# Attention scores of halves three to eight as two row tiles of the array, and a new order of the attention pieces

## The chip, the cores and the metric

The kernel runs on one core of a Trainium2 chip. The metric is the device time of one execution in microseconds; where several runs are given, it is their median. Before the change it is 242.2 us (three runs, 242.13 to 242.77). The profiled execution, from which all other times here are taken, has a span of 239.8 us.

Engines are called by the names of the profile: PE is the matrix engine (PEld its weight loads), ACT the engine for exponentials and other functions, DVE the vector engine, POOL the general engine, SP the queue that issues transfers.

## The reference

Attention over a window of 96 keys and 8 global keys, with a bias by distance, for 4 batches of 8 heads, 768 positions and 64 dimensions to a head; then a gated feed-forward (512 to 1536 to 512) over all 3072 rows.

```python
scores = (q @ k.T) / sqrt(64) + bias          # [4, 8, 768, 768]
keep   = (key < 8) | (0 <= row - key < 96)
a      = softmax(where(keep, scores, -1e9))
x      = (a @ v) as [3072, 512]
out    = (max(x @ w_gate, 0) * (x @ w_val)) @ w_out
```

## The kernel before

The work goes in eight halves (s = 0 to 7) of 384 rows: half of one batch's positions, all 8 heads. Halves 0 and 1 have a path of their own. From half 2 on, the attention of half c+1 is woven into the feed-forward of half c: a list of feed-forward items, each about 0.65 us of PE, and a list of attention pieces that are dropped between them at given fractions of the way.

The heads are handled in four pairs (p = 0 to 3). kT[b][p] holds the keys of both heads of a pair, head 0 in partitions 0 to 63 and head 1 in 64 to 127, as stationary matrices of 128 columns for each block j of keys. The queries of a pair are held twice in qTb, each copy with the other head's partitions set to zero, so that one product over all 128 partitions gives the scores of both heads side by side:

```python
qTb = [const.tile([128, HP, 2, QH], BF16, name=f"qT{i}") for i in range(2)]   # d, pair, head, row
qz  = [const.tile([128, NN, HP, 2, 128], BF16, name=f"qz{i}") for i in range(2)]  # zero-padded, before the transpose

def piece_qk(s, p, g, later=None):
    ...
    qd = qTb[s % 2][:, p].rearrange("d e (n p) -> d e n p", n=NN)
    bank = banks_of_half[half][g]                 # one or two blocks of keys
    ps = qk_psum.tile([128, 512], FP32, name="qk_ps")
    ...
    for j, a, w, m in bank:
        n_ = 2 * NN * w
        nc.tensor.matmul(ps[:, c : c + n_], lhsT=kt[:, j, :],
                         rhs=qd[:, :, :, a : a + w], start=True, stop=True)
        c += n_
    nc.scalar.activation(es[:, 0:cols], ps[:, 0:cols], AF.Exp, bias=0.0, scale=scale)
    ...                                           # piece_mask multiplies es by m_all, on DVE
```

A pair takes three such banks. Their products have 432, 432 and 288 + 48 columns in an even half, and 144 + 336, 384 + 96 and 432 in an odd half.

The product with the values is taken for one head at a time. Its output has the 64 value columns and, in the other 64 partitions, the sum of the weights; the reciprocal comes by a logarithm and an exponential, for both heads together:

```python
def piece_av(s, p, e):
    av = av_psum.tile([128, 512], FP32, name="av_ps")
    ...                                           # 4 (even) or 5 (odd) matmuls
    nc.scalar.activation(ln[o0 : o0 + 64], av[d0 : d0 + 64, 0:QH], AF.Ln, bias=0.0, scale=1.0)
    if e == 1:
        ...
        nc.scalar.activation(rc, ln, AF.Exp, bias=0.0, scale=-1.0)
        piece_norm(s, p, 0)                       # DVE: xT = av * rc, head 0; head 1 by a later piece
```

PSUM has eight banks: three for scores (qk_psum), two for these products (av_psum), three for the feed-forward (ff_psum). A bank is written again only when its last reader is done. The order of the attention pieces, and where they stand:

```python
        QK = lambda p: [(0.18, lambda g=g: qk(p, g)) for g in range(3)]
        AV = lambda p: [(0.29, lambda e=e: (flush(), piece_av(s, p, e))) for e in range(2)]
        N = lambda p: [(0.0, lambda: piece_norm(s, p, 1))]
        g = QK(3)
        a = AV(2)
        return (QK(0) + QK(1) + AV(0) + N(0) + QK(2) + AV(1) + N(1) + g[0:1] + a[0:1] + g[1:3] + a[1:2]
                + N(2) + [(0.0, lambda: None)] * 2 + AV(3) + N(3))
    ...
    placed.append(spread(attention_pieces(c + 1), 0.0, 0.88 if c + 2 < NHALF else 0.8))
```

The feed-forward of a half is 24 items (12 of gate, 12 of val, each four matmuls of 384 columns) and then, for half 6, seven items p1, p2, p4, p6, p5, p7, p3 of six matmuls of 256 columns (two row tiles multiplied in seven products in place of eight); halves 3 to 5 have four items of three matmuls of 512 columns ahead of these. Their results are combined on DVE from the PSUM banks b (p1), a (p2 and p6), d (p4 and p5), c (p7 and p3):

```python
            def p6():
                self.product(st["a"], DH, ss(2), tt(2))
                add(st["o"][:, 0:2], two(st["a"]), st["o"][:, 2:3].to_broadcast([128, 2, DH]))
            def p5():
                self.product(st["d"], DH, ss(1), tt(1))
                add(st["o"][:, 2:4], two(st["d"]), st["o"][:, 1:2].to_broadcast([128, 2, DH]))
            ...
            def p3():
                self.product(st["c"], DH, ss(4), bb(1, 1))
                second(st["c"][:, 0:DH])          # an add of 512 columns, and a store
                add(st["o"][:, 3], st["c"][:, DH:], st["o"][:, 3])
```

Halves 0 and 1 take the values' product in another form (piece_av_wide): stationary matrices of 64 columns, so that the products of the two heads lie in the left and right half of the array (128 x 64 in the profile's names). It is the only place, besides the transposes of half 1, where the kernel before uses a part of the array at a time.

Of the kernel before, what the change touches and what calls it, by code (L numbers as in the profile page):

```python
# [8 lines left out]
FP32 = mybir.dt.float32  # L9
BF16 = mybir.dt.bfloat16  # L10
FP16 = mybir.dt.float16
# [5 lines left out]
def kernel(  # L17
# [51 lines left out]
    es_pool = ctx.enter_context(tc.tile_pool(name="es", bufs=3))  # L69
# [17 lines left out]
    kT = [[const.tile([128, NT, 128], BF16, name=f"kT{i}_{p}") for p in range(HP)] for i in range(2)]  # L87
    qTb = [const.tile([128, HP, 2, QH], BF16, name=f"qT{i}") for i in range(2)]
    kNb = [const.tile([128, HP, QH], BF16, name=f"kN{i}") for i in range(2)]
    qz = [const.tile([128, NN, HP, 2, 128], BF16, name=f"qz{i}") for i in range(2)]  # L90
    kc = [const.tile([128, NN, DM], BF16, name=f"kc{i}") for i in range(2)]

    obuf = const.tile([128, 2, 5, DM // 2], FP32)
# [149 lines left out]
    def warm_up(n):  # L243
        wps = ff_psum.tile([128, 512], FP32, name="ff_ps")
        for _ in range(n):
            nc.tensor.matmul(wps, lhsT=warm, rhs=warm.unsqueeze(1).to_broadcast([128, 4, 128]), start=True, stop=True)

    xT_of = {}
    es_of = {}
    es01_of = {}  # L250
    av_of = {}

    cast_of = {}
# [91 lines left out]
    def piece_exp(s, p, g):  # L345
        if p == HP - 1:

            es = kNb[s].rearrange("d p t -> d (p t)")[:, 480 * g : 480 * (g + 1)]
        else:
            if g == 0:  # L350
                es01_of[s, p] = es_pool.tile([128, 2, 480], BF16, name="es01")
            es = es01_of[s, p][:, g] if g < 2 else es_pool.tile([128, 480], BF16, name="es2")
# [5 lines left out]
        nc.scalar.activation(es[:, 0:c], qk_of[s, p][g][:, 0:c], AF.Exp, bias=0.0, scale=scale)  # L358
# [3 lines left out]
        for g in range(3):  # L362
            piece_exp(s, p, g)

    def piece_cast_k(s, p):
        nc.gpsimd.tensor_copy(  # L366
            kc[s % 2].rearrange("t n (h d) -> t h n d", d=D)[:, 2 * p : 2 * p + 2],
            ks_of[s][:, 2 * p : 2 * p + 2, :].rearrange("t e (n d) -> t e n d", n=NN))

    def piece_cast_q(s, p):  # L370

        qsrc = qs_of[s][:, 2 * p : 2 * p + 2, :].rearrange("t e (n d) -> t e n d", n=NN)
        for e in range(2):
            nc.gpsimd.tensor_copy(qz[s % 2][:, :, p, e, 64 * e : 64 * e + 64], qsrc[:, e])

    def piece_xk(s, n):
        nc.sync.dma_start_transpose(
            out=kNb[s % 2][:, :, n * 128 : (n + 1) * 128], in_=kc[s % 2][:, n])

    def piece_xq(s, n):  # L380
        nc.sync.dma_start_transpose(
            out=qTb[s % 2].rearrange("d p e t -> d (p e) t")[:, :, n * 128 : (n + 1) * 128],
            in_=qz[s % 2][:, n].rearrange("t p e z -> t (p e z)"))

    def piece_order(s, p):
        b, half = divmod(s, 2)
        put_keys(nc.gpsimd.tensor_copy, nc.gpsimd.tensor_copy, kT[b % 2][p], kNb[s % 2][:, p], half)

    def early_pieces(s):
        out = [(0.0, lambda p=p: piece_cast_k(s, p)) for p in range(HP)]  # L390
        out += [(0.0, lambda n=n: piece_xk(s, n)) for n in range(NN)]
        out += [(0.0, lambda p=p: piece_cast_q(s, p)) for p in range(HP)]
        out += [(0.0, lambda n=n: piece_xq(s, n)) for n in range(NN)]
        out += [(0.0, lambda p=p: piece_order(s, p)) for p in range(HP)]
        return out

    def piece_qk(s, p, g, later=None):
        b, half = divmod(s, 2)
        kt = kT[b % 2][p]
        qd = qTb[s % 2][:, p].rearrange("d e (n p) -> d e n p", n=NN)  # L400
        bank = banks_of_half[half][g]
        cols = sum(2 * NN * w for _, _, w, _ in bank)
        ps = qk_psum.tile([128, 512], FP32, name="qk_ps")
        if g == 0:
            es01_of[s, p] = es_pool.tile([128, 2, 480], BF16, name="es01")
        es = es01_of[s, p][:, g] if g < 2 else es_pool.tile([128, 480], BF16, name="es2")
        c = 0
        for j, a, w, m in bank:
            n_ = 2 * NN * w
# [23 lines left out]
    def piece_av(s, p, e):  # L433
        b, half = divmod(s, 2)
        h = 2 * p + e
        vb = vbuf[b % 2]
        av = av_psum.tile([128, 512], FP32, name="av_ps")
        av_of[s, p, e] = av
        av3 = av[:, 0:QH].rearrange("d (n p) -> d n p", n=NN)
        todo = [t for bank in banks_of_half[half] for t in bank]  # L440
        for i, (j, a, w, m) in enumerate(todo):
            es, c = es_of[s, p, j, e]
            z0 = 2 * D * h + (D if e == 0 else 0)
            nc.tensor.matmul(av3[:, :, a : a + w],  # L444
                             lhsT=vb[:, j, z0 : z0 + 128],
                             rhs=es[:, c : c + NN * w].rearrange("k (n p) -> k n p", n=NN),
                             start=(i == 0), stop=(i == len(todo) - 1),
                             skip_group_check=True)
# [4 lines left out]
        nc.scalar.activation(ln[o0 : o0 + 64], av[d0 : d0 + 64, 0:QH], AF.Ln, bias=0.0, scale=1.0)  # L453
        if e == 1:
            if s not in xT_of:
                xT_of[s] = xt_pool.tile([128, N_DC, QH], BF16, name="xT")
            rc = rc_pool.tile([128, QH], FP32, name="rcp")
            nc.scalar.activation(rc, ln, AF.Exp, bias=0.0, scale=-1.0)  # L458
            av_of[s, p, "r"] = rc
            piece_norm(s, p, 0)  # L460
# [43 lines left out]
    def piece_mul_wide(s, p):  # L504
        if s not in xT_of:
            xT_of[s] = xt_pool.tile([128, N_DC, QH], BF16, name="xT")
        nc.vector.tensor_tensor(xT_of[s][:, p, :], av_of[s, p][1][:, 0:QH], av_of[s, p, "r"], op=ALU.mult)  # L507

    def attention_pieces(s):
        masks = []  # L510

        def qk(p, g):
            ready = masks[:]
            masks.clear()
            piece_qk(s, p, g, masks)
            for f in ready:
                f()

        def flush():
            for f in masks:  # L520
                f()
            masks.clear()

        QK = lambda p: [(0.18, lambda g=g: qk(p, g)) for g in range(3)]
        AV = lambda p: [(0.29, lambda e=e: (flush(), piece_av(s, p, e))) for e in range(2)]
        N = lambda p: [(0.0, lambda: piece_norm(s, p, 1))]
        g = QK(3)
        a = AV(2)
        return (QK(0) + QK(1) + AV(0) + N(0) + QK(2) + AV(1) + N(1) + g[0:1] + a[0:1] + g[1:3] + a[1:2]
                + N(2) + [(0.0, lambda: None)] * 2 + AV(3) + N(3))  # L530


    out_v = out.rearrange("(s p n) d -> s n p d", p=128, n=NN)
# [156 lines left out]
    def ffn_pieces(c):  # L690
# [63 lines left out]
        if c == NHALF - 2:  # L754
            return f1, pair.items({"1": late[0:2], "2": late[2:4]})

        space = qz[0].rearrange("t n p e z -> t (n p e z)").bitcast(FP16)
# [35 lines left out]

    for h in range(H):
        setup_sid(h)
    QKB, FFB, AVB = (qk_psum, "qk_ps"), (ff_psum, "ff_ps"), (av_psum, "av_ps")

    def AV(s, p, *pools):
        piece_av_wide(s, p, *pools)
        piece_norm_wide(s, p)  # L800
# [133 lines left out]
    for i in range(2):  # L934
        nc.gpsimd.memset(qz[i].rearrange("t n p e z -> t (n p e z)").bitcast(mybir.dt.uint32), 0)
    for j in range(NT):
        fill_ones(nc.gpsimd, 1, j)
    for p in range(HP):
# [3 lines left out]
    def T2_piece(p):  # L942
        piece_t(2, p, *QKB, apart=True)
        piece_copy_k(2, p)
        piece_copy_q(2, p, nc.scalar.copy)

    T2 = [(0.0, lambda p=p: T2_piece(p)) for p in range(HP)]
    weave(f1_1[G[0]] + f1_0[G[1]][4:] + f1_1[G[1]],
# [3 lines left out]
          spread(T2, 0.55, 0.95))  # L952
    sums_wo = [(0.0, f) for i in (0, 3) for f in weight_sums(i, i + 3)]
    weave(f1_0[G[2]] + f1_1[G[2]] + f2_0 + f2_1,
          spread(attention_pieces(2), 0.02, 0.8), spread(early_pieces(3), 0.1, 0.76),
          spread(sums_wo, 0.42, 0.76))
# [46 lines left out]
```

The softmax here doesn't subtract the row's maximum and nothing guards it: scores larger than these inputs give would overflow.

## Time and profile before

| | us |
|---|---|
| time, median of 3 | 242.2 |
| span of the profile | 239.8 |
| PE busy | 232.1 (97%) |
| DVE busy | 174.8 (73%) |
| ACT busy | 154.3 (64%) |
| POOL busy | 95.6 (40%) |
| score matmuls (qk_ps from qT and kT), 118 | 26.6 busy |
| exponentials of scores, 78 | 40.9, 534 ns each |
| mask products, 118 | 32.9, 322 ns each |
| gate and val matmuls, 768 | 155.4 busy, 326 ns each |

Busy time of a matmul contains its way through the array, which overlaps the next one; what a matmul costs PE is the distance from its start to the next start. PE's clock is granted in full during the whole span, but for its first slices.

### The profile page before, as it was taken

The numbers are of one execution on the slowest core, as the hardware profiler recorded it, in microseconds if no ns is written. First come the engines' busy times: TensorE is split into PE (matmuls) and PEld (weight loads), VectorE is DVE, ScalarE is ACT, GpSimd is POOL, SyncE is SP. The second block draws the span as 40 slices with busy tenths as digits, with TensorE's granted clock in tenths as the row PEclk, the third lists the DMA queues.
The fourth block names the chain that finished last, engine by engine and source line by source line (L and its number), as shares of the span: only waits on it lengthen the run. The fifth ranks groups of instructions, "written<-read, shape, count | busy, mean of one in ns | idle before, by whom it ended". The sixth has DMA issues, their size and how long they took to land.

```text
span 239.8 us, 5192 instructions
## 1 busy us (share of the span) xinstructions
PE 232.1 (97%) x1859; PEld 155.9 (65%) x1859; DVE 174.8 (73%) x443; ACT 154.3 (64%) x328; POOL 95.6 (40%) x213
## 2 busy tenths in 40 slices
PE   7889999999999999999999999999999999999992
PEld 3676756666558666766658666676658666866682
DVE  6878676767877778585985778675985867964783
ACT  7899856878662787548754787547764888433300
POOL 8998935915590068103484066502460000000000
PEclk9999999999999999999999999999999999999999
DMA  6999999997989946938569756929451200020004
GB/s 171 197 173 185 205 282 261 171 103 253 129 178 148 305 122 133 93 94 258 92 112 128 224 159 154 110 68 290 69 131 45 90 0 3 0 87 3 0 26 151
DMA packets 78329, 32.37 MB, mean 135 GB/s; under 512 B 55424, under 2 KB 76928, under 8 KB 78304
## 3 DMA queue, kind: packets, MB, share of 16 engines
q0 software_dynamic: 34896, 10.27, 38.1%
q1 hardware_dynamic: 43408, 21.78, 34.3%
q8 instruction: 14, 0.23, 0.4%
q14 instruction: 11, 0.09, 0.1%
HBM read 28.38 MB, written 6.29 MB: 145 GB/s over the span
## 4 chain that ended last, share of the span: by engine, by line
PE 89%; ACT 4%; DMA 2%; DVE 1%; SPq 1%; issue 0%; DVEq 0%; ACTq 0%
PE ff_ps L700 51%; PE ff_ps L590 15%; PE ff_ps L733 9%; PE qk_ps L410 6%; PE av_ps L444 6%; DMA qs<-in_q_dram 2%; ACT es L358 2%; SPq L116 1%; PE av_ps L479 1%; PE qk_ps L296 1%; ACT es L413 1%; PE qk_ps L479 1%; DVE obuf L601 0%; ACT kN L358 0%; ACT grelu L709 0%; DVE xT L507 0%
## 5 line engine op out<-in xcount | busy, mean ns | idle before, releaser
L700 PE MATMUL ff_ps<-xT,wv 128*128 128x384 bf16 x384 | 77.7, 326 | 0.1
L700 PE MATMUL ff_ps<-xT,wg 128*128 128x384 bf16 x384 | 77.7, 325 | 0.0
L709 ACT ACTIVATE grelu<-ff_ps 128x384 bf16<-128x384 f32 x96 | 46.9, 491 | 45.3 <-PE ff_ps L700 32.6
L716 DVE TENSOR_TENSOR ht<-ff_ps,grelu 128x384 f16<-128x384 f32 x96 | 53.1, 554 | 24.4 <-PE ff_ps L700 12.8
L700 PEld LDWEIGHTS <-wv 128*128 128x128 bf16 x384 | 36.2, 97 | 22.3 <-DMA wv<-in_moe_w_val_dram 0.4
L700 PEld LDWEIGHTS <-wg 128*128 128x128 bf16 x384 | 36.0, 97 | 20.9 <-issue 0.5
L464 DVE TENSOR_TENSOR xT<-av_ps,rcp 64x384 bf16<-64x384 f32 x48 | 26.7, 555 | 24.9 <-ACT rcp L458 24.0
L413 ACT ACTIVATE es<-qk_ps 128x432 bf16<-128x432 f32 (+2 forms) x78 | 40.9, 534 | 5.5 <-PE qk_ps L410 3.5
L428 DVE TENSOR_TENSOR es<-es,m_all 128x432 bf16<-128x432 bf16 (+5 forms) x118 | 32.9, 322 | 0.2
L366 POOL CAST kc<-ks 128x384 bf16<-128x384 f32 x20 | 9.4, 517 | 57.9 <-DMA ks<-in_k_dram 57.9
L453 ACT ACTIVATE lnd<-av_ps 64x384 f32<-64x384 f32 x48 | 23.3, 485 | 8.9 <-PE av_ps L444 8.5
L410 PE MATMUL qk_ps<-qT,kT 128*128 128x432 bf16 (+5 forms) x118 | 26.6, 286 | 0.1
L151 POOL DMA_DIRECT2D vbuf<-in_v_dram x29 | 24.8, 863 | 0.1
L601 DVE TENSOR_TENSOR obuf<-ff_ps,obuf 128x512 f32<-128x512 f32 (+1 forms) x35 | 20.5, 592 | 4.3 <-PE ff_ps L590 2.0
L733 PE MATMUL ff_ps<-wo_sb,ht 128*128 128x512 f16 x96 | 22.8, 378 | 0.0
L444 PEld LDWEIGHTS <-vbuf 128*128 128x128 bf16 x216 | 18.3, 98 | 6.8
L444 PE MATMUL av_ps<-es,vbuf 128*128 128x216 bf16 (+4 forms) x216 | 21.4, 226 | 0.0
L590 PEld LDWEIGHTS <-hsum 128*128 128x128 f16 x168 | 16.4, 98 | 2.0
L410 PEld LDWEIGHTS <-kT 128*128 128x128 bf16 x118 | 11.4, 98 | 7.7
L590 PE MATMUL ff_ps<-wo_sum,hsum 128*128 128x256 f16 x126 | 14.9, 273 | 0.0
L590 PEld LDWEIGHTS <-ht 128*128 128x128 f16 x144 | 13.7, 97 | 1.8
L733 PEld LDWEIGHTS <-ht 128*128 128x128 f16 x96 | 8.7, 97 | 8.7
(125 smaller groups left out, 245.7 us busy)
## 6 DMA issues: line engine op xcount, KB each, us to landing
out_dram<-obuf SPq DMA_DIRECT2D x22, 256.0 KB
ks<-in_k_dram SPq DMA_DIRECT2D x5, 768.0 KB
qs<-in_q_dram SPq DMA_DIRECT2D x5, 768.0 KB
vbuf<-in_v_dram POOLq DMA_DIRECT2D x23, 120.0 KB, 4.8
wv<-in_moe_w_val_dram POOLq DMA_DIRECT2D x3, 512.0 KB, 9.8
wo_sb<-in_moe_w_out_dram POOLq DMA_DIRECT2D x1, 1536.0 KB, 21.1
wg<-in_moe_w_gate_dram POOLq DMA_DIRECT2D x2, 512.0 KB, 9.7
ks<-in_k_dram SPq DMA_DIRECT2D x4, 192.0 KB
```

The lines of the kernel that those rows point to most:

```text
L151: nc.gpsimd.dma_start(out=v_dst(b, NG + r0, NG + r0 + n, j), in_=v[b, :, KT * j + r0 : KT * j + r0 + n, :].rearrange("h p d -> p h d"))
L410: nc.tensor.matmul(ps[:, c : c + n_], lhsT=kt[:, j, :], rhs=qd[:, :, :, a : a + w], start=True, stop=True)
L413: nc.scalar.activation(es[:, 0:cols], ps[:, 0:cols], AF.Exp, bias=0.0, scale=scale)
L428: nc.vector.tensor_mul(e4, e4, mk)
L444: nc.tensor.matmul(av3[:, :, a : a + w], lhsT=vb[:, j, z0 : z0 + 128], rhs=es[:, c : c + NN * w].rearrange("k (n p) -> k n p", n=NN), star ...
L453: nc.scalar.activation(ln[o0 : o0 + 64], av[d0 : d0 + 64, 0:QH], AF.Ln, bias=0.0, scale=1.0)
L464: nc.vector.tensor_tensor(xT_of[s][r, p, :], av_of[s, p, e][r, 0:QH], av_of[s, p, "r"][r], op=ALU.mult)
L590: nc.tensor.matmul(ps[:, c0 : c0 + DH], lhsT=lhs(i), rhs=rhs(i), start=(i == 0), stop=(i == NP - 1), skip_group_check=True)
L700: nc.tensor.matmul(st[key][:, 0:QH], lhsT=w_of(w, dc, fc), rhs=xT_of[c][:, dc, :], start=(dc == 0), stop=(dc == N_DC - 1))
L709: nc.scalar.activation(gr, psg[:, 0:QH], AF.Relu, bias=0.0, scale=1.0)
L716: nc.vector.tensor_tensor(ht[:, fc, :], psv[:, 0:QH], st["r", fc], op=ALU.mult)
L733: nc.tensor.matmul(ps2, lhsT=ht[:, fc, n * 128 : (n + 1) * 128], rhs=wo_sb[:, fc, :], start=(fc == 0), stop=(fc == N_FC - 1))
```

## The change

The scores of halves 2 to 7 are no longer taken over all 128 partitions with zeros. The queries are held once, without padding; each product takes the 64 partitions of one head, keys and queries alike, so that the two heads of a pair use the upper and the lower half of the array's rows, and each product has half the columns. The two heads go to different banks, and a bank holds the same head of two neighbouring pairs. A "unit" of scores is written at once to four banks, one of av_psum and three of qk_psum; three units make up a half. Exponentials and masks are as many and as large as before.

```diff
-    qz = [const.tile([128, NN, HP, 2, 128], BF16, name=f"qz{i}") for i in range(2)]
+    qT2 = [qTb[1].rearrange(...)[:, i * HP * QH : (i + 1) * HP * QH].rearrange("d (p t) -> d p t", p=HP) for i in range(2)]
+    qc = [const.tile([128, NN, DM], BF16, name=f"qc{i}") for i in range(2)]
...
+    def score_unit(s, groups, pools):
+        for pp, g in groups:
+            banks = []
+            for e in range(2):
+                pool, name = pools.pop(0)
+                banks.append(pool.tile([128, 512], FP32, name=name))
+            c = 0
+            for j, a, w, m in banks_of_half[half][g]:
+                for p in (2 * pp, 2 * pp + 1):
+                    for e in range(2):
+                        r = slice(64 * e, 64 * e + 64)
+                        q3 = qT2[s % 2][r, p].rearrange("d (n p) -> d n p", n=NN)
+                        nc.tensor.matmul(banks[e][:, c : c + NN * w], lhsT=kT[b % 2][p][r, j, :],
+                                         rhs=q3[:, :, a : a + w], start=True, stop=True)
+                    c += NN * w
...
-        return (QK(0) + QK(1) + AV(0) + N(0) + QK(2) + AV(1) + N(1) + g[0:1] + a[0:1] + g[1:3] + a[1:2]
-                + N(2) + [(0.0, lambda: None)] * 2 + AV(3) + N(3))
+        U = [([(0, 0), (0, 1)], (AVB, QKB, QKB, QKB)),
+             ([(0, 2), (1, 0)], (AVB, QKB, QKB, QKB)),
+             ([(1, 1), (1, 2)], (AVB, QKB, QKB, QKB))]
+        return (X(U[0]) + X() + X() + X() + wait + X(U[1]) + X() + X() + a0[0:1] + X() + a0[1:2] + N(0) + wait
+                + X(U[2]) + X() + a1[0:1] + X() + X() + a1[1:2] + N(1) + wait * 2 + AV(2) + N(2) + wait * 2
+                + AV(3) + N(3))
...
-          spread(attention_pieces(2), 0.02, 0.8), ...
+          spread(attention_pieces(2), 0.02, 0.86), ...
-            placed.append(spread(attention_pieces(c + 1), 0.0, 0.88 if c + 2 < NHALF else 0.8))
+            placed.append(spread(attention_pieces(c + 1), 0.0, 0.92))
```

X is one exponential (with the unit's products ahead of it where one is named) and the masks of the exponential before; wait is an empty place. The list has 30 places where it had 26, and it ends later in the feed-forward.

The rest follows from the queries being held once: four casts of 384 columns on POOL for a half's queries in place of eight of 192, transposes of 512 columns by the DMA queue in place of 1024, one copy in place of two for each pair of half 2 on ACT, no zeroing of the padded buffers on POOL, and the space of the padded buffer that the last sums used is now that of qTb[0]. The pool of exponentials has 12 tiles, all those of a half, in place of three and three.

More of the change, by code (lines that the diff above doesn't have):

```diff
@@ L68 @@
     stage = ctx.enter_context(tc.tile_pool(name="stage", bufs=1))
-    es_pool = ctx.enter_context(tc.tile_pool(name="es", bufs=3))
+    es_pool = ctx.enter_context(tc.tile_pool(name="es", bufs=12))
     rc_pool = ctx.enter_context(tc.tile_pool(name="rc", bufs=2))
@@ L89 @@
     kNb = [const.tile([128, HP, QH], BF16, name=f"kN{i}") for i in range(2)]
-    qz = [const.tile([128, NN, HP, 2, 128], BF16, name=f"qz{i}") for i in range(2)]
+    qT2 = [qTb[1].rearrange("d p e t -> d (p e t)")[:, i * HP * QH : (i + 1) * HP * QH].rearrange(
+        "d (p t) -> d p t", p=HP) for i in range(2)]
+    qc = [const.tile([128, NN, DM], BF16, name=f"qc{i}") for i in range(2)]
     kc = [const.tile([128, NN, DM], BF16, name=f"kc{i}") for i in range(2)]
@@ L246, in warm_up @@
             nc.tensor.matmul(wps, lhsT=warm, rhs=warm.unsqueeze(1).to_broadcast([128, 4, 128]), start=True, stop=True)
+    QKB, FFB, AVB = (qk_psum, "qk_ps"), (ff_psum, "ff_ps"), (av_psum, "av_ps")
     xT_of = {}
     es_of = {}
-    es01_of = {}
     av_of = {}
@@ L349, in piece_exp @@
         else:
-            if g == 0:
-                es01_of[s, p] = es_pool.tile([128, 2, 480], BF16, name="es01")
-            es = es01_of[s, p][:, g] if g < 2 else es_pool.tile([128, 480], BF16, name="es2")
+            es = es_pool.tile([128, 480], BF16, name="es")
         c = 0
@@ L363, in piece_biased, with piece_cast2, piece_x @@
             piece_exp(s, p, g)
-    def piece_cast_k(s, p):
+    def piece_cast2(s, p, dst, src):
         nc.gpsimd.tensor_copy(
[L367 to L383, printed above, removed]
+            dst[s % 2].rearrange("t n (h d) -> t h n d", d=D)[:, 2 * p : 2 * p + 2],
+            src[s][:, 2 * p : 2 * p + 2, :].rearrange("t e (n d) -> t e n d", n=NN))
+    def piece_x(dst, src, n):
+        nc.sync.dma_start_transpose(out=dst[:, :, n * 128 : (n + 1) * 128], in_=src[:, n])
     def piece_order(s, p):
@@ L389, in early_pieces @@
     def early_pieces(s):
[L390 to L393, printed above, removed]
+        out = [(0.0, lambda p=p: piece_cast2(s, p, kc, ks_of)) for p in range(HP)]
+        out += [(0.0, lambda n=n: piece_x(kNb[s % 2], kc[s % 2], n)) for n in range(NN)]
+        out += [(0.0, lambda p=p: piece_cast2(s, p, qc, qs_of)) for p in range(HP)]
+        out += [(0.0, lambda n=n: piece_x(qT2[s % 2], qc[s % 2], n)) for n in range(NN)]
         out += [(0.0, lambda p=p: piece_order(s, p)) for p in range(HP)]
@@ L403, in piece_qk @@
         ps = qk_psum.tile([128, 512], FP32, name="qk_ps")
-        if g == 0:
-            es01_of[s, p] = es_pool.tile([128, 2, 480], BF16, name="es01")
-        es = es01_of[s, p][:, g] if g < 2 else es_pool.tile([128, 480], BF16, name="es2")
+        es = es_pool.tile([128, 480], BF16, name="es")
         c = 0
@@ L507, in piece_mul_wide, with unit_exp, mask @@
         nc.vector.tensor_tensor(xT_of[s][:, p, :], av_of[s, p][1][:, 0:QH], av_of[s, p, "r"], op=ALU.mult)
-    def attention_pieces(s):
[L510 to L517, printed above, removed]
+    def score_unit(s, groups, pools):
+        b, half = divmod(s, 2)
+        out = []
+        for pp, g in groups:
[3 more added lines that the diff above has]
+                banks.append(pool.tile([128, 512], FP32, name=name))
+                out.append((pp, g, e, banks[e]))
+            c = 0
[7 more added lines that the diff above has]
+                    c += NN * w
+        return out
+    def unit_exp(s, pp, g, e, ps):
+        bank = banks_of_half[s % 2][g]
+        cols = sum(2 * NN * w for _, _, w, _ in bank)
+        es = es_pool.tile([128, 480], BF16, name="es")
+        nc.scalar.activation(es[:, 0:cols], ps[:, 0:cols], AF.Exp, bias=0.0, scale=scale)
+        def mask():
+            c = 0
+            for j, a, w, m in bank:
+                n_ = 2 * NN * w
+                e4 = es[:, c : c + n_].rearrange("k (i n p) -> k i n p", i=2, n=NN)
+                h0 = 4 * pp + e
+                mk = m_all[:, h0 : h0 + 3 : 2, 0 if j == 0 else 1, :, m : m + w]
+                if w == WQ:
+                    e4 = e4.rearrange("k i n p -> k i (n p)")
+                    mk = mk.rearrange("k i n p -> k i (n p)")
+                nc.vector.tensor_mul(e4, e4, mk)
+                for i in range(2):
+                    es_of[s, 2 * pp + i, j, e] = (es, c + i * NN * w)
+                c += n_
+        return mask
+    def attention_pieces(s):
+        masks, units = [], []
         def flush():
@@ L522, in flush, with scores, x @@
             masks.clear()
-        QK = lambda p: [(0.18, lambda g=g: qk(p, g)) for g in range(3)]
-        AV = lambda p: [(0.29, lambda e=e: (flush(), piece_av(s, p, e))) for e in range(2)]
-        N = lambda p: [(0.0, lambda: piece_norm(s, p, 1))]
-        g = QK(3)
-        a = AV(2)
-        return (QK(0) + QK(1) + AV(0) + N(0) + QK(2) + AV(1) + N(1) + g[0:1] + a[0:1] + g[1:3] + a[1:2]
-                + N(2) + [(0.0, lambda: None)] * 2 + AV(3) + N(3))
+        def scores(groups, pools):
+            units.extend(score_unit(s, groups, list(pools)))
+        def x(scored=None):
+            ready = masks[:]
+            masks.clear()
+            if scored:
+                scores(*scored)
+            masks.append(unit_exp(s, *units.pop(0)))
+            for f in ready:
+                f()
+        U = [([(0, 0), (0, 1)], (AVB, QKB, QKB, QKB)),
+             ([(0, 2), (1, 0)], (AVB, QKB, QKB, QKB)),
+             ([(1, 1), (1, 2)], (AVB, QKB, QKB, QKB))]
+        X = lambda u=None: [(0.0, lambda: x(u))]
+        AV = lambda p: [(0.0, lambda e=e: (flush(), piece_av(s, p, e))) for e in range(2)]
+        N = lambda p: [(0.0, lambda: piece_norm(s, p, 1))]
+        wait = [(0.0, lambda: None)]
+        a0, a1 = AV(0), AV(1)
+        return (X(U[0]) + X() + X() + X() + wait + X(U[1]) + X() + X() + a0[0:1] + X() + a0[1:2] + N(0) + wait
+                + X(U[2]) + X() + a1[0:1] + X() + X() + a1[1:2] + N(1) + wait * 2 + AV(2) + N(2) + wait * 2
+                + AV(3) + N(3))
     out_v = out.rearrange("(s p n) d -> s n p d", p=128, n=NN)
@@ L755, in ffn_pieces @@
             return f1, pair.items({"1": late[0:2], "2": late[2:4]})
-        space = qz[0].rearrange("t n p e z -> t (n p e z)").bitcast(FP16)
+        space = qTb[0].rearrange("d p e t -> d (p e t)").bitcast(FP16)
         across = Pair((c - 1, 2), (c, 2), space.rearrange("t (s c z) -> t s c z", s=4, c=NP))
@@ L795 @@
         setup_sid(h)
-    QKB, FFB, AVB = (qk_psum, "qk_ps"), (ff_psum, "ff_ps"), (av_psum, "av_ps")
     def AV(s, p, *pools):
@@ L933 @@
     nc.gpsimd.memset(vbuf[1][:, NT - 1, :].bitcast(mybir.dt.uint32), 0)
-    for i in range(2):
-        nc.gpsimd.memset(qz[i].rearrange("t n p e z -> t (n p e z)").bitcast(mybir.dt.uint32), 0)
     for j in range(NT):
@@ L944, in T2_piece @@
         piece_copy_k(2, p)
-        piece_copy_q(2, p, nc.scalar.copy)
+        nc.scalar.copy(qT2[0][:, p], tp_of[2, p, 0])
     T2 = [(0.0, lambda p=p: T2_piece(p)) for p in range(HP)]
@@ L954 @@
     weave(f1_0[G[2]] + f1_1[G[2]] + f2_0 + f2_1,
-          spread(attention_pieces(2), 0.02, 0.8), spread(early_pieces(3), 0.1, 0.76),
+          spread(attention_pieces(2), 0.02, 0.86), spread(early_pieces(3), 0.1, 0.76),
           spread(sums_wo, 0.42, 0.76))
```

## The prediction

> **What bounds the kernel now.** I read the page's busy shares first, then the chain of work that ended last, then PE's waits, and last the timeline of single stretches.
>
> ```profile
> PE 232.1 (97%) x1859; PEld 155.9 (65%) x1859; DVE 174.8 (73%) x443; ACT 154.3 (64%) x328; POOL 95.6 (40%) x213
> ...
> PE 89%; ACT 4%; DMA 2%; DVE 1%; SPq 1%; issue 0%; DVEq 0%; ACTq 0%
> PE ff_ps L700 51%; PE ff_ps L590 15%; PE ff_ps L733 9%; PE qk_ps L410 6%; PE av_ps L444 6%; DMA qs<-in_q_dram 2%; ACT es L358 2%; SPq L116 1%; PE av_ps L479 1%; PE qk_ps L296 1%; ACT es L413 1%; PE qk_ps L479 1%; DVE obuf L601 0%; ACT kN L358 0%; ACT grelu L709 0%; DVE xT L507 0%
> ```
>
> The first line alone could mislead, for a matmul's busy time overlaps the next one's. The chain settles it: 89% of the span is PE following PE, from about 22 us to 235 us. So a PE column that goes away between these times shortens the run, and relief of ACT, DVE, POOL or the transfers is worth nothing as long as no wait appears. The score products (L410) are 6% of the chain. The timeline of half 5's feed-forward shows how tightly PE runs, start to start (the columns are start, duration, instruction; the duration overlaps the next start):
>
> ```profile
> 158.47 0.81 PE L700 MATMUL ff_ps<-xT,wg 128*128 128x384 bf16 x4
> 159.12 0.35 PE L410 MATMUL qk_ps<-qT,kT 128*128 128x432 bf16 x1
> 159.30 0.81 PE L700 MATMUL ff_ps<-xT,wv 128*128 128x384 bf16 x4
> 159.95 0.35 PE L410 MATMUL qk_ps<-qT,kT 128*128 128x432 bf16 x1
> 160.14 0.81 PE L700 MATMUL ff_ps<-xT,wg 128*128 128x384 bf16 x4
> 160.79 0.31 PE L410 MATMUL qk_ps<-qT,kT 128*128 128x288 bf16 x2
> 160.94 0.81 PE L700 MATMUL ff_ps<-xT,wv 128*128 128x384 bf16 x4
> ```
>
> Four of 384 columns take 0.65 us, 0.1625 each: 384 columns at 2.4 per ns are 0.160, and 2.5 ns are left over. A score product of 432 takes 0.18. In the whole stretch from 30 to 235 us I find only five starts that come more than 0.04 us late, about 0.5 us together.
>
> **What the Trainium skill says.** (1) "TensorE: Matmul & The Clock Gate", section "Back-to-back issue gap", gives N/2.4 + 2.5 ns for isolated matmuls; the trace above agrees (0.1625 us at N = 384). (2) The same page, "Part 3: Packing small matmuls — row/col tiling", says that matmuls with different row groups run at once, starting about 4 ns apart, so that two products over 64 rows cost little more than one. The kernel before has no row tiles to show it, but it has column tiles in half 1, and those do overlap (next fence). (3) "TensorEngine Tiling (Array Packing)", section "Key Properties", says that changing the tiling mode drains the engine. The trace agrees and gives the price. (4) The same page, "Gotcha 1: PSUM Pressure", wants row tiles in different banks; the change gives each head its own.
>
> ```profile
> 25.20 0.50 PE L479 MATMUL av_ps<-es,ones 128*64 128x72 bf16 x10
> 25.54 0.48 PE L479 MATMUL av_ps<-es,vbuf 128*64 128x72 bf16 x10
> 25.85 0.48 PE L479 MATMUL qk_ps<-es,ones 128*64 128x72 bf16 x10
> 26.16 0.48 PE L479 MATMUL qk_ps<-es,vbuf 128*64 128x72 bf16 x10
> 26.57 1.47 PE L700 MATMUL ff_ps<-xT,wv 128*128 128x384 bf16 x8
> 27.88 0.81 PE L700 MATMUL ff_ps<-xT,wg 128*128 128x384 bf16 x4
> 28.62 0.50 PE L479 MATMUL av_ps<-es,ones 128*64 128x72 bf16 x10
> ```
>
> Each ten are five pairs of 72, 192, 168, 48 and 216 columns, 696 to a side. One after the other they would need 1392/2.4 = 0.58 us; they take 0.31 (25.54 to 25.85). So halves of the array do work at once. The modes: 27.88 to 28.62 is 0.74 for four products that need 0.65, so 0.09 to enter; the first ten take 0.34 and not 0.31, 0.03 more; 26.16 to 26.57 is 0.41 and not 0.31, so 0.10 to leave. A round trip costs 0.22 us.
>
> **The change part by part.** *Removed on PE:* in an even half a pair's scores take 0.18 + 0.19 + 0.15 = 0.52 us (starts above), in an odd half 0.59 (0.21 + 0.20 + 0.18, from the same view at 76.75 to 78.64). Four pairs and three halves of each: 12 × 0.52 + 12 × 0.59 = 13.3 us.
>
> *Added on PE:* with the heads at once, an even half's pair needs columns 216, 216, 144, 24: 0.0925 + 0.0925 + 0.0625 + 0.028 = 0.275. An odd half's has exactly the five sizes of the fence above, 0.31. 12 × 0.275 + 12 × 0.31 = 7.0 us. So the columns give 6.3 us.
>
> *Mode changes:* a half has three units, each with one entry and one exit; six halves make 18, at 0.22 us: 4.0 us. This assumes that row tiles drain as column tiles do. It takes most of the gain, 2.3 us are left. It also shows why units are gathered over four banks: with twelve visits to a half it would be 72 × 0.22 = 16 us.
>
> *Weight loads:* there are 216 instead of 108, each 128 columns wide, where column tiles load 64. A 48-column product before, with its own load, starts its successor 0.03 us later, so a load needs no more than that; a pair of loads may need 0.06 where the smallest pairs have 0.025 to 0.03. One such pair in even, two in odd halves: at most 12 × 0.03 + 12 × 0.06 = 1.1 us. I take 0.4 and have 1.9 left.
>
> *ACT and DVE:* 12 exponentials of 534 ns and as many mask products of 322 ns to a half as before. Half 2's query copies fall from eight of 472 ns (3.8 us) to four of about 0.5 (1.8 us saved) on ACT, POOL's casts from eight of 385 ns to four of about 517 (1 us less to a half), its zeroing of 2.7 us goes. None is on the chain: zero.
>
> **The waits that may come** decide the rest.
>
> At the end of half 6's feed-forward the attention now ends late. Instruction order: the last value product of head 1 comes after p6; then p5, p7, p3, 18 products of 0.109 us, 1.96 us, and half 7's gate, whose fourth product needs the last pair of xT 0.49 us later. How long that takes is seen before, at the same place:
>
> ```profile
> 205.67 0.47 PE L444 MATMUL av_ps<-es,vbuf 128*128 128x72 bf16 x5
> 206.18 0.48 ACT L453 ACTIVATE lnd<-av_ps 64x384 f32<-64x384 f32 x1 [0.26 <-PE av_ps L444]
> 206.69 0.52 ACT L458 ACTIVATE rcp<-lnd 128x384 f32<-128x384 f32 x1
> 207.25 0.55 DVE L464 TENSOR_TENSOR xT<-av_ps,rcp 64x384 bf16<-64x384 f32 x1 [0.43 <-ACT rcp L458]
> ...
> 209.45 2.74 DVE L601 TENSOR_TENSOR obuf<-ff_ps,obuf 128x512 f32<-128x512 f32 x4
> ```
>
> From the product's end (0.31 us after its start, 205.98) to the first scaled head it is 1.8 us. After it DVE, which works in order, does p5's add (0.69) and then the second head (0.55): 3.1 us, against 2.45 that PE has: 0.6 us of waiting. p3's adds follow, and the third product of half 7 wants their bank: some 0.3 more. Call it 0.9 us, where before the same place lost 0.09.
>
> In halves 2 to 5 the same end has one item more behind it, 3.1 us against 3.1, but the adds of p5 and p3 come behind the two scalings and hold the banks of the next half's first val and second gate: 0.2 us each, 0.8 us in all.
>
> Elsewhere I find the slack just positive. The third unit wants the bank of pair 0's first head three items (1.95 us) after the second head's product; that takes 1.8 as above. The second unit comes five items (3.25 us) after the first, in which ACT has four exponentials and two or three relus, about 3.1 us. Sum of the waits: 0.9 + 0.8 + 0.2 for these, less 0.3 of the 0.5 us that PE loses now = 1.6 us; since the places look chosen by trial, I take 0.7 of it.
>
> Sum: 242.2 − 1.9 + 0.7 = 241.0 us.
>
> **The rivals.** *Row tiles need no drain.* Then 6 us come off and the time is 236 to 237. Against it stands the drain at every change of column tiles in this trace, both ways; for it, that no row tile was measured. *The waits win.* ACT and DVE have 18 to 20 us of work in each half's 25 to 27 us, more in its first two thirds, where a unit's four banks now come in a burst; if each unit waits 0.2 us more (18 × 0.2 = 3.6), the time is 243 to 244. For it: the two slacks of 0.15 us; against it: the empty places stand just there. *The tiles do not overlap*, because the two write 128 partitions each of PSUM at a time, twice what column tiles do: then 13.3 us stay, the drains come on top, and it is 246 or more. The page on TensorE speaks against it, the trace has nothing on it. *Other engines' relief pays*: nothing in the chain speaks for it.
>
> **Range and chances.** The mode change is the largest uncertain term: at half its price the time is 239.0, at one and a half 243.0. Waits add 1 us either way. I take 238.8 to 243.0 for 8 times in 10. Faster by over 2% needs under 237.4 us, hardly possible unless the drain is absent: 0.07. Slower by over 2%, above 247.0, needs tiles that don't overlap: 0.02. Within 2%: 0.91.
>
> **What would show it.** In the changed trace: pairs of score products that start a few ns apart, a pair of 216 columns to a next start of 0.09 us; a unit of an even half of about 0.4 to 0.6 us with 0.2 us of excess at its edges, and 7.0 us of columns in all; PE's waits at half 7's first gate, about 0.6 us, and at the starts of the halves. If the edges show no excess the first rival holds; if units begin late, waiting for ACT, the second; if the two of a pair start 0.09 us apart, the third.

## The result and the profile after

The changed kernel takes 240.67 us (median of four runs, 240.22 to 241.15) against 242.31 us; the ratio is 0.9933, with a 95% interval of 0.9913 to 0.9953. It is faster by 1.6 us, with an uncertainty of some 0.5 us. A second set of six runs gave 240.65 us and 0.9935 (0.9915 to 0.9955).

From the page of the changed kernel, busy shares and chain:

```profile
PE 229.8 (96%) x1967; PEld 152.4 (64%) x1967; DVE 173.7 (73%) x443; ACT 149.5 (63%) x324; POOL 90.3 (38%) x191
...
PE 81%; ACT 6%; DMA 6%; DVE 3%; POOL 1%; issue 1%; SPq 0%; DVEq 0%
PE ff_ps L742 49%; PE ff_ps L632 14%; PE ff_ps L775 9%; PE av_ps L431 5%; DMA wv<-in_moe_w_val_dram 4%; PE av_ps L513 2%; PE qk_ps L513 2%; ACT es L359 2%; DMA qs<-in_q_dram 1%; POOL vbuf L154 1%; ACT obuf L263 1%; ACT lnd L440 1%; DVE obuf L643 1%; DVE xT L451 1%; ACT rcp L445 1%
```

The score products (L513, before L410) fell from 6% of the chain to 4%, and PE from 89% to 81%. The DMA entry of 4% lies at 20.3 to 30.3 us, ahead of the changed part: in this run the weights of val arrive last there, and PE goes on at 30.33 us, in the kernel before at 30.10. New in the changed part are the entries of ACT and DVE at its later lines (L440, L445, L451, L643): there are now places where PE waits for them. A unit of an odd half, from the timeline of half 2's feed-forward (start, duration, instruction):

```profile
75.94 0.81 PE L742 MATMUL ff_ps<-xT,wg 128*128 128x384 bf16 x4
76.69 0.20 PE L513 MATMUL av_ps<-qT,kT 64*128 64x72 bf16 x1
76.69 0.20 PE L513 MATMUL qk_ps<-qT,kT 64*128 64x72 bf16 x1
76.73 0.20 PE L513 MATMUL av_ps<-qT,kT 64*128 64x72 bf16 x1
76.73 0.20 PE L513 MATMUL qk_ps<-qT,kT 64*128 64x72 bf16 x1
76.76 0.23 PE L513 MATMUL av_ps<-qT,kT 64*128 64x168 bf16 x1
76.77 0.23 PE L513 MATMUL qk_ps<-qT,kT 64*128 64x168 bf16 x1
76.84 0.23 PE L513 MATMUL av_ps<-qT,kT 64*128 64x168 bf16 x1
76.84 0.45 PE L513 MATMUL qk_ps<-qT,kT 64*128 64x168 bf16 x9
77.22 0.82 PE L742 MATMUL ff_ps<-xT,wv 128*128 128x384 bf16 x4
```

Three things stand in it. The two heads' products, one to av_ps and one to qk_ps, start together. Sixteen products of 1920 columns in all take 0.53 us (76.69 to 77.22) where 1920/2.4 would be 0.80. And four gate products that need 0.65 us occupy 0.75 (75.94 to 76.69): 0.10 to enter the tiles.

I took the same reading over all products of halves 2 to 7. The distance from one start to the next is columns/2.4 + 2.5 ns (the granted clock is 1.00 from end to end in both traces); what exceeds it is put down to the edges of a unit or to a late start:

| us on PE, halves 2 to 7 | before | after |
|---|---|---|
| columns of the score products | 13.3 | 7.2 |
| entering and leaving tiles | 0 | 18 × 0.195 = 3.5 |
| late starts (waits) | 0.5 | 2.0 |
| sum | 13.8 | 12.7 |

The sum gives 1.1 us. The traces agree: from the first val product behind half 1's attention (30.10 us before, 30.33 after) to PE's last start (235.32 and 234.51) it is 205.22 us before and 204.18 after. The medians differ by 1.6 us. Part of the rest lies outside the span from first to last instruction: an execution of the kernel before takes some 2.1 us more than its span (241.88 and 239.8), one of the changed kernel 1.8 (240.77 and 239.0). Beside the second set of six runs, the median span before is 240.0 us against 238.9, 1.1 us apart again. Why the time outside the span differs, no run shows.

Most of the waits lie in two places, both at the end of half 6's feed-forward. From the timeline of the changed kernel, first place:

```profile
202.60 0.81 PE L742 MATMUL ff_ps<-xT,wv 128*128 128x384 bf16 x4
203.01 0.48 ACT L440 ACTIVATE lnd<-av_ps 64x384 f32<-64x384 f32 x1
203.25 1.36 PE L632 MATMUL ff_ps<-wo_sb,ht 128*128 128x256 f16 x11
203.53 0.52 ACT L445 ACTIVATE rcp<-lnd 128x384 f32<-128x384 f32 x1
204.08 0.55 DVE L451 TENSOR_TENSOR xT<-av_ps,rcp 64x384 bf16<-64x384 f32 x1 [1.21 <-ACT rcp L445]
204.56 0.54 DVE L758 TENSOR_TENSOR ht<-ff_ps,grelu 128x384 f16<-128x384 f32 x1
205.15 0.28 PE L632 MATMUL ff_ps<-wo_sb,ht 128*128 128x256 f16 x1 [0.54 <-DVE ht L758]
```

The last val of half 6 is done on PE at 203.25, and its product with the relu (L758) could follow. DVE has ahead of it the scaling of half 7's third pair (L451), which stands idle 1.21 us for the reciprocal. Only then does L758 run, and the twelfth product of the output, which reads it, starts at 205.15; eleven products had been issued by 204.34 and the next was due at 204.45, so 0.70 us are lost. Second place, five microseconds later:

```profile
207.91 0.52 ACT L445 ACTIVATE rcp<-lnd 128x384 f32<-128x384 f32 x1
208.46 0.55 DVE L451 TENSOR_TENSOR xT<-av_ps,rcp 64x384 bf16<-64x384 f32 x1 [0.63 <-ACT rcp L445]
208.94 0.67 DVE L643 TENSOR_TENSOR obuf<-ff_ps,obuf 128x512 f32<-128x512 f32 x1
209.16 0.65 PE L742 MATMUL ff_ps<-xT,wg 128*128 128x384 bf16 x3
209.64 0.56 DVE L451 TENSOR_TENSOR xT<-av_ps,rcp 64x384 bf16<-64x384 f32 x1
210.25 0.32 PE L742 MATMUL ff_ps<-xT,wg 128*128 128x384 bf16 x1 [0.45 <-DVE xT L451]
```

Half 7's gate has issued three of its four products and waits 0.61 us for the last pair's second head, which stands behind p5's add on DVE. This is the order that the prediction had read: reciprocal, first head, add, second head.

The other waits are small: 0.07 and 0.18 us at two units of scores, whose av_psum bank a scaling on DVE (L451) frees too late, four of 0.09 at the first output product of halves 2 to 5, and one of 0.09 behind half 7's first gate.

### The profile page after: what moved, and what is told of

Read it like the earlier page. It is cut to its first block, busy times and chain, and to the rows that moved or that the text cites. A ratio compares the mean times of both kernels' runs of the same rounds, so it can differ in the third digit from the quotient of the medians.

```text
span 239.0 us, 5383 instructions
## 1 busy us (share of the span) xinstructions
PE 229.8 (96%) x1967; PEld 152.4 (64%) x1967; DVE 173.7 (73%) x443; ACT 149.5 (63%) x324; POOL 90.3 (38%) x191
## 4 chain that ended last, share of the span: by engine, by line
PE 81%; ACT 6%; DMA 6%; DVE 3%; POOL 1%; issue 1%; SPq 0%; DVEq 0%
PE ff_ps L742 49%; PE ff_ps L632 14%; PE ff_ps L775 9%; PE av_ps L431 5%; DMA wv<-in_moe_w_val_dram 4%; PE av_ps L513 2%; PE qk_ps L513 2%; ACT es L359 2%; DMA qs<-in_q_dram 1%; POOL vbuf L154 1%; ACT obuf L263 1%; ACT lnd L440 1%; DVE obuf L643 1%; DVE xT L451 1%; ACT rcp L445 1%
## 5 line engine op out<-in xcount | busy, mean ns | idle before, releaser
L758 DVE TENSOR_TENSOR ht<-ff_ps,grelu 128x384 f16<-128x384 f32 x96 | 53.3, 556 | 27.3 <-PE ff_ps L742 24.0
L451 DVE TENSOR_TENSOR xT<-av_ps,rcp 64x384 bf16<-64x384 f32 x48 | 26.6, 554 | 22.2 <-ACT rcp L445 21.1
L440 ACT ACTIVATE lnd<-av_ps 64x384 f32<-64x384 f32 x48 | 23.3, 485 | 17.8 <-PE av_ps L431 17.1
L367 POOL CAST kc<-ks 128x384 bf16<-128x384 f32 x20 | 10.2, 553 | 55.5 <-DMA ks<-in_k_dram 48.1
L534 DVE TENSOR_TENSOR es<-es,m_all 128x432 bf16<-128x432 bf16 (+3 forms) x108 | 30.3, 321 | 0.8 <-ACT es L522 0.7
L522 ACT ACTIVATE es<-qk_ps 128x432 bf16<-128x432 f32 (+2 forms) x54 | 27.8, 530 | 0.1
L775 PE MATMUL ff_ps<-wo_sb,ht 128*128 128x512 f16 x96 | 23.6, 378 | 0.0
L643 DVE TENSOR_TENSOR obuf<-ff_ps,obuf 128x512 f32<-128x512 f32 (+1 forms) x35 | 20.4, 589 | 3.4 <-PE ff_ps L632 0.8
L632 PEld LDWEIGHTS <-ht 128*128 128x128 f16 x144 | 13.8, 98 | 3.4 <-DVE ht L758 0.8
L445 ACT ACTIVATE rcp<-lnd 128x384 f32<-128x384 f32 x24 | 12.5, 523 | 0.8
L632 PE MATMUL ff_ps<-wo_sb,ht 128*128 128x256 f16 x96 | 12.0, 273 | 0.5 <-DVE ht L758 0.5
```

The source lines that it names most:

```text
L451: nc.vector.tensor_tensor(xT_of[s][r, p, :], av_of[s, p, e][r, 0:QH], av_of[s, p, "r"][r], op=ALU.mult)
L534: nc.vector.tensor_mul(e4, e4, mk)
L632: nc.tensor.matmul(ps[:, c0 : c0 + DH], lhsT=lhs(i), rhs=rhs(i), start=(i == 0), stop=(i == NP - 1), skip_group_check=True)
L643: add = lambda o, x, y: nc.vector.tensor_tensor(o, x, y, op=ALU.add)
L758: nc.vector.tensor_tensor(ht[:, fc, :], psv[:, 0:QH], st["r", fc], op=ALU.mult)
L775: nc.tensor.matmul(ps2, lhsT=ht[:, fc, n * 128 : (n + 1) * 128], rhs=wo_sb[:, fc, :], start=(fc == 0), stop=(fc == N_FC - 1))
```

## The experiments

The theory: columns bring 6 us, the tiling mode takes 3.5 back, a late end of the attention takes another 1.5. The first three runs test the first two terms. "Changed kernel" is 240.67 us.

**All 128 rows, same schedule.** Heads are not kept apart: each score is the sum of both heads'.

```diff
-                        r = slice(64 * e, 64 * e + 64)
+                        r = slice(0, 128)
```

> The changed kernel with its schedule, banks and number of score products as they are, but each product taken over all 128 partitions, so that there are no row tiles; it leaves out the separation of the two heads (their scores are summed). Theory: the 0.2 us of excess at each of the 18 units is the change of tiling mode; without tiles it goes (3.5 us less), while the columns come one after another (13.5 us instead of 7.2, 6.3 us more): 2.8 us slower than the changed kernel, about 243.5 us. Rival: the excess at the edges is a wait for four banks; then it stays, and the kernel is 6.3 us slower, 247 us.

Measured: 244.29 us, ratio to the kernel before 1.0079 (1.0052 to 1.0105). From its timeline, the same unit:

```profile
75.96 0.81 PE L742 MATMUL ff_ps<-xT,wg 128*128 128x384 bf16 x4
76.61 0.20 PE L513 MATMUL av_ps<-qT,kT 128*128 128x72 bf16 x1
76.64 0.20 PE L513 MATMUL qk_ps<-qT,kT 128*128 128x72 bf16 x1
...
76.96 0.66 PE L513 MATMUL qk_ps<-qT,kT 128*128 128x168 bf16 x9
77.46 0.81 PE L742 MATMUL ff_ps<-xT,wv 128*128 128x384 bf16 x4
```

75.96 to 76.61 is 0.65: the excess at the edge is gone, with the same banks, the same waits and the same products. Over the 18 units the excess at the edges is 0.44 us, all of it at two units that wait for a bank (0.17 and 0.27), where it was 3.6 with these waits in it. The columns, one after the other, cost 13.9 us instead of 7.2. That makes 6.7 us more and some 3.3 less; the medians are 3.6 us apart. The 0.2 us at each unit are the mode and not the banks. The run also shows what the new order and the later end cost without the tiles: it is 2.2 us slower than the kernel before, in its trace some 1.7 by late starts and 0.6 by columns, which now come in 216 products in place of 108.

**Both heads on the same rows.** The second head's own scores are left out.

```diff
-                        r = slice(64 * e, 64 * e + 64)
+                        r = slice(0, 64)
```

> The changed kernel with both heads' products taken over partitions 0 to 63, still as row tiles and in two banks; it leaves out the second head's own scores. Theory: two products overlap only because they use different rows of the array; on the same rows they follow each other, columns 13.5 us instead of 7.2, edges as before: 6.3 us slower than the changed kernel, about 247 us. Rival: a product over 64 rows is by itself cheap, whichever rows it uses: no difference, 240.7 us.

Measured: 248.06 us, ratio 1.0232 (1.0196 to 1.0269), 7.4 us above the changed kernel. Its timeline:

```profile
77.73 0.81 PE L742 MATMUL ff_ps<-xT,wg 128*128 128x384 bf16 x4
78.48 0.20 PE L513 MATMUL av_ps<-qT,kT 64*128 64x72 bf16 x1
78.52 0.20 PE L513 MATMUL qk_ps<-qT,kT 64*128 64x72 bf16 x1
78.55 0.20 PE L513 MATMUL av_ps<-qT,kT 64*128 64x72 bf16 x1
...
79.43 0.82 PE L742 MATMUL ff_ps<-xT,wv 128*128 128x384 bf16 x4
```

Here the entry costs 0.10 (77.73 to 78.48 is 0.75), and the products stand 0.03 us apart instead of together. A product over 64 rows is not cheaper than one over 128; the gain is only that two of them, on different rows, go at once. Over the 18 units the columns cost 14.0 us in place of 7.2, and the edges are 3.6 us as before. From 31.04 us, where val goes on here, to PE's last start the trace is 6.9 us longer than the changed kernel's; the rest of the 7.4 us lies ahead of the changed part or between single runs. The three kernels separate the two effects: mode without overlap, neither, both.

**Twice the visits.** Each unit is taken as two units of two banks, one place apart.

```diff
-        U = [([(0, 0), (0, 1)], (AVB, QKB, QKB, QKB)), ...
+        U = [([g], (QKB if i % 2 else AVB, QKB))
+             for i, g in enumerate(((0, 0), (0, 1), (0, 2), (1, 0), (1, 1), (1, 2)))]
-        return (X(U[0]) + X() + X() + X() + wait + X(U[1]) + X() + X() ...
+        return (X(U[0]) + X(U[1]) + X() + X() + wait + X(U[2]) + X(U[3]) + X() ...
```

> The changed kernel with each unit of four banks taken in two visits of two banks, one place apart; the products, exponentials and masks are the same. Theory: each visit pays for entering and leaving the tiling mode, 0.2 us; with about 36 visits instead of 18 the kernel is 3.5 us slower, about 244.2 us. Rival: the excess is a wait for banks, which smaller visits ease: no slower, 240.7 us or less.

Measured: 244.64 us, ratio 1.011 (1.0077 to 1.0143), 4.0 us above the changed kernel. In the trace the 36 visits have 7.3 us of excess at their edges where 18 had 3.6, waits included. The columns stay at some 7.3 us. So the price is one per visit, with half as much in each.

**The waits: the first head's scaling one place later, for half 7's last two pairs.**

```diff
-            piece_norm(s, p, 0)                      # right behind the reciprocal
+            if s < NHALF - 1 or p < 2:
+                piece_norm(s, p, 0)
-        N = lambda p: [(0.0, lambda: piece_norm(s, p, 1))]
+        N = lambda p: [(0.0, lambda: [piece_norm(s, p, e) for e in ((1,) if s < NHALF - 1 or p < 2 else (0, 1))])]
```

> The changed kernel, but for half 7's third and fourth pair the first head's scaling on DVE is issued one place later, together with the second head's. Theory: the two waits at the end of half 6's feed-forward (0.7 us in its first product of the output, 0.6 us in half 7's first gate) come from DVE standing still in order behind a reciprocal; behind the other work it does no harm: 1.0 to 1.3 us faster than the changed kernel, about 239.5 us. Rival: the attention simply ends too late, and the last pair is scaled no earlier: only the first 0.7 us or nothing, 240.0 to 240.7 us.

Measured: 239.95 us, ratio 0.9911 (0.9884 to 0.9937), 0.7 us below the changed kernel. The intervals of the two overlap, and 0.7 us is also what the rival gave for the first wait alone, so the trace has to decide. The first of the two places:

```profile
202.76 0.81 PE L743 MATMUL ff_ps<-xT,wv 128*128 128x384 bf16 x4
203.41 1.47 PE L633 MATMUL ff_ps<-wo_sb,ht 128*128 128x256 f16 x12
203.68 0.56 DVE L759 TENSOR_TENSOR ht<-ff_ps,grelu 128x384 f16<-128x384 f32 x1 [0.65 <-ACT lnd L440]
203.68 0.52 ACT L445 ACTIVATE rcp<-lnd 128x384 f32<-128x384 f32 x1
204.24 1.14 DVE L452 TENSOR_TENSOR xT<-av_ps,rcp 64x384 bf16<-64x384 f32 x2
```

The product of relu and val now runs while ACT makes the reciprocal, the twelve output products go without a break, and both heads are scaled by 205.38, where the changed kernel had them at 205.69, though its last val starts 0.16 us sooner. At the second place the wait fell from 0.61 to 0.17 us. All late starts together fell by 1.1 us, and PE's last product starts 0.98 us sooner, though val went on 0.13 us later at 30.46. The theory holds, not the rival: with the same late end, the other order on DVE takes away the first wait and most of the second.

**The old ends.** The changed kernel with the places of the kernel before (0.8, 0.88 and 0.8 in place of 0.86, 0.92 and 0.92).

> The changed kernel with the attention pieces spread as before the change (to 0.8 in the first stage, 0.88 in the middle, 0.8 in half 6), so closer together. Theory: the late end of half 6 costs 1.3 us, which go, but closer places bring waits for banks of 0.1 to 0.3 us a half: between 0.5 us faster and 0.5 us slower than the changed kernel, 240.2 to 241.2 us. Rival: the banks' slack is larger than thought: 1.3 us faster, 239.4 us. Second rival: the slack is smaller, each unit waits: over 1 us slower, above 241.7 us.

Measured: 239.94 us, ratio 0.9903 (0.9877 to 0.993), 0.7 us below the changed kernel. The two waits of the end are gone, so an earlier end removes them as well as the other order does; in their place half 7's third unit of scores is late by 0.37 us and the third unit of halves 3 to 6 by 0.04 to 0.07 each. The result lies between the theory and its first rival: closer places do bring bank waits, as the slack of 0.15 us had it, but smaller ones than the late end brings.

**The late end, on the kernel before** (its places spread to 0.86, 0.92 and 0.92).

> The kernel before with its attention pieces spread as far as in the changed kernel (to 0.86, 0.92, 0.92). Theory: the late end costs the kernel before as much as the changed one: 0.7 to 1.3 us slower than the kernel before, about 243.3 us. Rival: the waits belong to the new order of pieces, not to the end: no difference, 242.3 us.

Measured: 244.26 us, ratio 1.0089 (1.0063 to 1.0114), 2.2 us slower than the kernel before. This is more than expected. The two large waits lie at the same two places: 0.58 us in half 6's first output products, behind the same product of relu and val, and 0.52 us behind half 7's first gate, here for an add on DVE that has the bank. Four more, of 0.30 to 0.33 us, stand at the first val of halves 3 to 6: each waits for its bank, which a DVE add for the half before still reads (the one that PE starts at 104.80 us had its add from 104.05 us on). This is the wait that the prediction expected there in the changed kernel. Seven starts late by 0.04 to 0.20 us, 0.7 us in all, have no cause shown. So such waits come with the late end and the order of DVE, also without row tiles.

**Mixtures, for a faster kernel.** The changed kernel was run again beside them:

> The changed kernel itself once more, beside the three that follow, as their measure: 240.7 us by its first runs.

Measured: 240.65 us, ratio 0.9935 (0.9915 to 0.9955).

Late scaling and one empty place of half 7 moved ahead of its third unit:

```diff
-    a0[1:2] + N(0) + wait + X(U[2]) ...  a1[1:2] + N(1) + wait * 2 + AV(2)
+    a0[1:2] + N(0) + wait * (1 if s < NHALF - 1 else 2) + X(U[2]) ...
+    a1[1:2] + N(1) + wait * (2 if s < NHALF - 1 else 1) + AV(2)
```

> The late scaling of half 7's third and fourth pair, and for half 7 one empty place moved from behind its second pair to ahead of its third unit of scores, which began 0.18 us late. Theory: both waits go, 1.0 + 0.2 us faster than the changed kernel, 239.5 us. Rival: the place that is missing behind the second pair makes a new wait of the same size: 1.0 us faster, 239.7 us.

Measured: 239.81 us, ratio 0.9902 (0.9882 to 0.9922); its six runs, 239.71 to 240.0, all lie below the six of the changed kernel on the same chip (240.22 to 241.01). The rival was right about the place: the unit's wait went (0.18), and new ones of 0.14 and 0.40 us came at the third pair's products. This is nonetheless the fastest kernel of the study by its median, 0.84 us below the changed one and 2.3 below the one before; it is not told apart from the late scaling alone (239.95) or from the old ends (239.94).

The same, with half 6's attention ended at 0.88:

> As the run before, but half 6's attention spread to 0.88 in place of 0.92, so that the last pair is scaled earlier. Theory: the 0.17 us that remain at half 7's first gate go too, 239.3 us. Rival: closer places bring back the wait at the third unit: 239.7 us.

Measured: 240.12 us, ratio 0.9913 (0.9891 to 0.9936). Neither: both heads' scalings again come ahead of the last product of relu and val on DVE, and the wait of 0.56 us in the output products is back.

**Two units of six banks.**

```diff
-        U = [([(0, 0), (0, 1)], (AVB, QKB, QKB, QKB)), ...
+        U = [([(pp, 0), (pp, 1), (pp, 2)], (FFB, QKB, QKB, QKB, AVB, AVB)) for pp in range(2)]
-        return (X(U[0]) + X() + X() + X() + wait + X(U[1]) ...
+        return (X(U[0]) + X() * 5 + wait + AV(0) + N(0) + wait + AV(1) + N(1) + wait * 2
+                + X(U[1]) + X() * 5 + wait + AV(2) + N(2) + wait + AV(3) + N(3))
```

> The changed kernel with two units of six banks to a half (one bank of ff_psum, three of qk_psum, two of av_psum) in place of three of four, so 12 visits in place of 18. Theory of the mode change: 6 visits less, 1.2 us faster, if no bank is waited for: 239.5 us. Rival: a unit of six banks finds them occupied and waits, 0.2 us or more at each of 12 visits, and the feed-forward lacks its third bank: 240.7 us or more.

Measured: 243.54 us, ratio 1.0056 (1.0037 to 1.0074), 2.9 us above the changed kernel. The rival holds. Leaving the tiles costs 1.0 us in all instead of 1.6, a third less, as 12 visits should; but the late starts (those of units counted whole) add up to 6.3 us where the changed kernel has 2.2. From its timeline, the start of half 4's first unit:

```profile
104.21 0.81 PE L739 MATMUL ff_ps<-xT,wg 128*128 128x384 bf16 x4
105.37 0.25 PE L513 MATMUL ff_ps<-qT,kT 64*128 64x216 bf16 x1 [0.35 <-DVE obuf L640]
```

The unit begins with the bank of ff_psum, whose last reader is an add of the half before on DVE; 1.16 us pass from the gate's start where 0.65 + 0.10 are needed.

## Why the prediction was right

Predicted were 241.0 us, 238.8 to 243.0; measured 240.67. By its own steps:

- *Columns: 6.3 us less.* Right: 13.3 to 7.2, with the weight loads, for which 0.4 were set aside, inside it: 7.0 was reckoned for the columns alone, so loads and small products cost 0.2.
- *Mode changes: 18 × 0.22 = 4.0 us.* Right in kind, and nearly in size: 18 × 0.195 = 3.5. The price read from column tiles of half 1 held for row tiles, and two experiments show that it is the mode: without tiles it goes, with twice the visits it doubles.
- *Half 7's first gate, 0.6 us.* Right to 0.01; the following 0.3 were 0.09.
- *Starts of halves 3 to 6, 0.2 us each.* Wrong: nothing there. The unit of scores that stands between the first gate and the first val, 0.57 us with its edges, seems to give DVE's add its time: in the kernel before with late ends one bank of scores of some 0.2 us stood there, and the wait came. In the changed kernel the first output product of halves 2 to 5 is 0.09 late, four times.
- *Elsewhere, the slack is just positive, 0.2 us.* Right at the units of scores (0.25), and wrong at the first output products of half 6, where 0.70 us are lost. I had followed the last pair's scaling through DVE's order, not the third pair's.
- *The sum of the waits, 1.6 us, of which I took 0.7.* The sum was 1.5 above the kernel before, so the discount "since the places look chosen by trial" was unfounded: the run with the old ends is 0.7 us faster. The errors, 0.5 less for the mode, 0.2 less for columns and loads and 0.8 more for waits, nearly cancel. That the sum of the terms comes out within 0.1 us of the trace is luck; that columns gain, edges cost and late starts decide the rest is not.
- *Rivals.* No drain: refuted, the edges are there. Tiles that don't overlap: refuted by the pairs' starts and by the run on the same rows. Waits win: they took 1.5 us, not 3.6 or more. Relief of ACT, DVE and POOL: ACT's busy time fell from 154.3 to 149.5 us and POOL's from 95.6 to 90.3, and PE's own account covers the difference of the traces, and of the median spans, without it. The 0.5 us between that and the medians' difference are within the uncertainty; some 0.3 of them lie outside the span, and their cause stays open.

## What to carry to other kernels

Two products over half the rows each, on different rows, halve the columns' time (here each had its own bank; one bank for both was not tried); each visit to the tiles costs a fixed price (here 0.2 us), so gather products into few visits, but only as far as the banks are free when the visit begins. An engine that works in order must not be given an instruction that waits, ahead of one that is ready and that the bound engine needs: moving it one place took 1.1 us of late starts from PE, where the tiling, its price paid, gives 2.6. And read every instruction near a stage's end through the in-order queue, not only the last one.

## What the runs showed of the hardware

Entering the tiles costs 95 to 97 ns at 16 of the 18 units; at the other two PE waits for a bank. The weight loads of the changed kernel at the entry above show where this time lies:

```profile
76.11 0.26 PEld L742 LDWEIGHTS <-wg 128*128 128x128 bf16 x2
76.68 0.49 PEld L513 LDWEIGHTS <-kT 64*128 64x128 bf16 x16 [0.32 <-issue]
```

Elsewhere in the stream a load stands one product ahead (the one of 76.11 is for the product of 76.27). The first load of the tiles starts with its own product, at 76.68, 0.25 us after the start of the last gate product (76.43). At half 7's third unit the bank is not yet free:

```profile
193.60 0.65 PE L742 MATMUL ff_ps<-xT,wg 128*128 128x384 bf16 x3
194.18 0.29 PEld L513 LDWEIGHTS <-kT 64*128 64x128 bf16 x4 [0.32 <-issue]
194.36 0.24 PE L513 MATMUL av_ps<-qT,kT 64*128 64x192 bf16 x1
```

The last of the three gate products starts at 193.92. The first load comes the same 0.25 us later, at 194.18, and only the product waits, until 194.36: the entry passes during the wait. The run over all 128 rows agrees. At the two units that wait for a bank, the start is 0.166 and 0.276 us late with tiles and 0.168 and 0.268 without. So at these two units the entry costs nothing more; the exit's 0.08 to 0.09 was not examined so.

Many short waits of PE are nearly as long as an entry, 0.09 us, but a load that is held back does not explain them: at half 2's first output product, 0.09 us late, the load stands ahead (94.46, the product at 94.71). What sets that size no run here shows.
